# Fused attention and mixture of experts: the gates' spread earlier in GpSimd's order, two weight tiles behind the attention, four small products fewer

## The chip, the cores and the metric

One core of a Trainium2 chip runs the whole program. The metric is the device time in microseconds; a kernel is run several times and the median counts. TensorE (PE in the profile) multiplies, VectorE (DVE), ScalarE (ACT) and GpSimd (POOL) work element by element, and SyncE (SP), GpSimd and ScalarE issue DMAs, which 16 DMA engines carry out.

## The reference

Causal attention by blocks over 8 batches, 8 heads, 576 positions and a head size of 64, and then a layer of 8 experts, each of which keeps at most `capacity` = 80 of the 4608 tokens that chose it:

```python
mask = block_i >= block_j                      # blocks of 64 positions
scores = np.where(mask, q @ k.T / 8, -1e9)
x = softmax(scores) @ v                        # then reshaped to [4608, 512]
logits = x @ w_gate                            # 8 experts
expert_idx = argmax(logits); gate_w = softmax(logits)[expert_idx]
for e in range(8):
    tok_idx = the (at most 80) tokens of expert e with the largest gate_w
    h = np.maximum(x[tok_idx] @ w1[e], 0.0)
    out[tok_idx] = gate_w[tok_idx, None] * (h @ w2[e])
```

All other rows of the output are zero.

## The kernel before

**Attention.** A step of the loop in line 764 handles one pair of heads; four pairs are a batch, so 32 pairs run in software pipelining. The list `TURN` (line 35) is an order written out by hand: entry `(d, what, ...)` in step i does `what` for pair i + d, and each engine runs its own instructions in the order of the list. `scores` (L607) makes the products of q and k, `max` (L643) and `soft` (L652) the softmax on VectorE and ScalarE, `back` (L682, L690) transposes the probabilities P on TensorE, `take` (L739, L741) copies them out of PSUM, `values` (L731, L709) multiplies by v.

**Loads.** `prep 0` transposes q on VectorE (L585) and scales it on GpSimd (L588). GpSimd also issues the DMAs of `load_v` (L554 and L557, three for the pair two ahead), of `load_k` (L544, four for the pair five ahead) and of `store` and `store2` (L353, two each, x of a finished batch into the DRAM tensor `xs`). An engine runs its instructions in order, so an issue or a wait on GpSimd holds all behind it. q, zeros for the output and, later, most weights are issued by SP.

**Gates.** Once a batch is complete its gates are worked out in pieces spread over the next steps: `logits0`, `lt`, `lm`, `ga`, `gexp`, `gb`, which ends in `Gm` (L443) on VectorE. Then `gturn` (L451) on GpSimd spreads `Gm` into `sp`, one instruction of 128x320 elements, and in the following step `turn2` (L466) multiplies `sp` on TensorE, in front of `values`. In the step where `gturn` stands, its entry comes behind `load_v`, `load_k`, `store` and `store2`. The last batch does this on VectorE instead.

**Experts.** Four weight tiles of 2 MB are loaded by GpSimd during the last four steps (L304). The others are loaded by SP in four parts each (L309), in the order in which the experts need them; every part waits for the part three before it (`UNDERWAY` = 3), and `weights(n, after)` lets its n tiles wait for the DMA `after`. Line 842 loads one tile once the last store of x has landed; line 1046 loads four more once the second gather has.

**Selection.** Between attention and experts the 80 best tokens of each expert are found. Twelve "picks" (L941) multiply one-hot rows `OH`, made on VectorE and GpSimd (L936), by token numbers; behind each of the first eight picks stands a product of the identity with itself (`warm`, L751) that nothing reads. The picks' sum gives the indices `gi` (L959) and eight indirect DMAs (L952) gather the tokens' rows of `xs`; one gather of row 0, whose result is overwritten, precedes them. Then each expert runs: transposes (L1079), first product (L1066 into `ps`), second product (L1066 into `av`), transposes back (L1109), scatter (L1114).

Of the kernel before, what the change touches and what calls it, by code (L numbers as in the profile page):

```python
# [21 lines left out]
FW0, FWA, FWC, FWB = 4, 3, 1, 1  # L22
# [48 lines left out]
    (1, "soft", 4, 0),  # L71
    (0, "soft", 0, 0),
    (0, "back", "B"),
    (2, "load_v"),
    (5, "load_k"),
    (-3, "store"),
    (-4, "store2"),
    (-4, "gate", "gturn"),
    (0, "back", "A"),
    (-1, "take", "values", 0),  # L80
    (2, "prep", 1),
# [59 lines left out]
def tile_attn_moe(ctx, tc, q, k, v, w_gate, w1, w2, capacity, out, xs=None, dbg=None):  # L141
# [153 lines left out]
    def weights(n, after=None, parts=PARTS):  # L295

        nonlocal nw
        for _ in range(n):
            src, e = wlist[nw]
            w_ = wpools[nw % len(wpools)].tile([P, KP * F], F32, name="w")  # L300
            nw += 1
            wt_[src is w2, e] = w_ = w_.rearrange("p (a f) -> p a f", f=src.shape[2])
            if nw <= FW0:
                nc.gpsimd.dma_start(w_, src[e].rearrange("(a p) f -> p a f", p=P))  # L304
                continue
            view = src[e].rearrange("(a p) f -> p a f", p=P)
            na = w_.shape[1]
            for a in range(0, na, na // parts):
                load = nc.sync.dma_start(w_[:, a:a + na // parts], view[:, a:a + na // parts]).ins  # L309
                for before in ((after,) if after is not None else ()) + tuple(parts_[-UNDERWAY:][:1] if len(parts_) >= UNDERWAY else ()):  # L310
                    tc.add_manual_dep(load, before.name, mybir.DependencyInfo(
                        mybir.DependencyClass.Sync, mybir.DependencyReason.DATA))
                parts_.append(load)
# [429 lines left out]
    def warm(n, wt, after=None, w=identr, c=4):  # L743

        if not n:
            return
        with ExitStack() as order:
            if after is not None:
                order.enter_context(tc.issue_after(after.ins))
            for i in range(n):  # L750
                nc.tensor.matmul(wt[:, 0:c * P].rearrange("p (a c) -> p a c", c=P), lhsT=w,  # L751
                                 rhs=w.unsqueeze(1).broadcast_to([P, c, P]), start=(i == 0), stop=(i == n - 1))
# [7 lines left out]
    with tc.manual_schedule():  # L760
# [48 lines left out]
        bt = batches[B - 1]  # L809
# [29 lines left out]
    tw = dict(reuse_waits="tile")  # L839
    fwa = late.enter_context(tc.tile_pool(name="fwa", bufs=FWA, **right, **tw))  # L840
    wpools += [fwa] * FWA
    weights(1, bt.stored.ins)
    sel2 = late.enter_context(tc.tile_pool(name="sel2", bufs=1, **right, **tw))


# [41 lines left out]
    HOLD = 1  # L887
# [45 lines left out]
    for n_, i in enumerate((*range(NV), *range(NH, NCAND), *range(NV, NH))):  # L933
        quiet = NH <= i < NH + NQ
        with ExitStack() if quiet else tc.issue_after(counted.ins):
            made = (pool if quiet else vec).tensor_scalar(  # L936
                OH[:, i], iota_b[:, int(i >= NV)], scalar1=pen[:, i:i + 1], scalar2=cnt[:, i:i + 1],
                op0=ALU.subtract, op1=ALU.is_equal)
        if quiet:
            last_made = made  # L940
        picked = nc.tensor.matmul(pick[0:CHUNK, 0:3 * E], lhsT=OH[:, i], rhs=RI[:, i].rearrange("p k e -> p (k e)"),  # L941
                                  start=(n_ == 0), stop=(n_ == NCAND - 1))
        if n_ < 8:
            warm(1, wt[:, n_ % 2], picked, c=2)
    gi = sel2.tile([CHUNK, E], I32, name="gi")

# [4 lines left out]
    def fetch(e, index):  # L951
        return pool.indirect_dma_start(  # L952
            out=xg[e], out_offset=None, in_=xs[:, :], in_offset=bass.IndirectOffsetOnAxis(ap=index.bitcast(U32), axis=0),
            bounds_check=NTOK - 1, oob_is_err=False).ins
# [5 lines left out]
    fetches = [fetch(e, gi[:, e:e + 1]) for e in range(E)]  # L960
# [82 lines left out]
    fwc = late.enter_context(tc.tile_pool(name="fwc", bufs=FWC, **right, **tw))  # L1043
    fwb = late.enter_context(tc.tile_pool(name="fwb", bufs=FWB, **tw))
    wpools += [fwc] * FWC + [fwb] * FWB
    weights(FWA - 1 + FWC + FWB, fetches[HOLD])

    def divide(dst, src, a0=0, a1=NP):

# [309 lines left out]
```

## Time and profile before

| what | value |
|---|---|
| median of 3 runs | 431.2 us (430.88 to 433.99) |
| the profiled execution's own time | 432.01 us |
| its span, first to last instruction | 430.3 us |
| TensorE busy | 391.5 us, 91% of the span |
| ScalarE busy | 275.3 us, 64% |
| VectorE busy | 269.8 us, 63% |
| GpSimd busy | 226.1 us, 53% |
| mean granted clock of TensorE | 0.973 |

The profile is of one execution. Busy time doesn't count DMA issues, though an engine can do nothing else while it issues one. "A <- B" in a row of waits means that A stood idle until B was done; in an instruction's row the bracket gives the idle time before it. The attention takes the span up to about 309 us, the selection up to 328, the experts the rest.

### The profile page before, as it was taken

The numbers are of one execution on the slowest core, as the hardware profiler recorded it, in microseconds if no ns is written. First come the engines' busy times: TensorE is split into PE (matmuls) and PEld (weight loads), VectorE is DVE, ScalarE is ACT, GpSimd is POOL, SyncE is SP. The second block draws the span as 40 slices with busy tenths as digits, with TensorE's granted clock in tenths as the row PEclk, the third lists the DMA queues.
The fourth block names the chain that finished last, engine by engine and source line by source line (L and its number), as shares of the span: only waits on it lengthen the run. The fifth ranks groups of instructions, "written<-read, shape, count | busy, mean of one in ns | idle before, by whom it ended". The sixth has DMA issues, their size and how long they took to land.

```text
span 430.3 us, 15486 instructions
## 1 busy us (share of the span) xinstructions
PE 391.5 (91%) x6355; PEld 296.6 (69%) x6355; DVE 269.8 (63%) x583; ACT 275.3 (64%) x796; POOL 226.1 (53%) x370
## 2 busy tenths in 40 slices
PE   8999979979979996996999799999996899999892
PEld 4667747757756774774677576767663799899892
DVE  4778759958976895897789689888683122111111
ACT  2999959959995996999699799999420110111000
POOL 8787734874674588558448855653367300000001
PEclk9999989989999999999999999999999699999997
DMA  9999945995595599769769974799957999899931
GB/s 141 156 154 150 147 107 129 224 211 127 142 195 141 133 207 171 164 136 204 175 134 205 177 181 130 181 352 327 299 155 241 313 286 308 283 315 316 314 100 35
DMA packets 120060, 84.59 MB, mean 197 GB/s; under 512 B 94333, under 2 KB 96381, under 8 KB 119984
## 3 DMA queue, kind: packets, MB, share of 16 engines
q1 hardware_dynamic: 103040, 45.57, 44.9%
q0 software_dynamic: 15744, 37.68, 36.1%
q8 instruction: 52, 0.85, 0.8%
q10 hardware_dynamic: 1200, 0.30, 0.3%
q14 instruction: 24, 0.20, 0.2%
HBM read 63.38 MB, written 20.33 MB: 195 GB/s over the span
## 4 chain that ended last, share of the span: by engine, by line
PE 65%; POOL 11%; DVE 8%; DMA 6%; SPq 4%; issue 3%; ACT 1%; POOLq 0%; ACTq 0%; DVEq 0%
PE sc L731 17%; PE sc L607 14%; PE ps L1066 11%; PE av L1066 7%; PE sc L682 7%; DVE negm L643 4%; POOL ld L544 4%; SPq L544 3%; PE sc L370 2%; POOL vn L557 2%; POOL xs L353 2%; DMA vn<-in_v_dram 1%; DVE T L585 1%; PE sc L690 1%; POOL T L588 1%
## 5 line engine op out<-in xcount | busy, mean ns | idle before, releaser
L652 ACT ACTIVATE P<-sc,negm 128x320 f32<-128x320 f32 (+4 forms) x320 | 163.8, 528 | 13.0 <-DVE negm L643 7.0
L643 DVE TENSOR_REDUCE negm<-sc 128x1 f32<-128x448 f32 (+4 forms) x224 | 128.9, 624 | 22.2 <-PE sc L614 15.0
L607 PE MATMUL sc<-T,T 64*128 64x64 f32 (+4 forms) x768 | 110.6, 414 | 1.5 <-ACT T L581 0.5
L607 PEld LDWEIGHTS sc<-T,T 64*128 64x128 f32 x768 | 69.4, 187 | 33.1 <-issue 25.3
L544 POOL DMA_DIRECT2D ld<-in_k_dram x120 | 80.2, 678 | 0.0
L739 ACT COPY PT<-sc 128x1024 f32<-128x1024 f32 x63 | 60.7, 1018 | 21.9 <-PE sc L682 21.4
L588 POOL TENSOR_SCALAR T<-T 128x576 f32<-128x576 f32 x31 | 20.6, 666 | 91.8 <-DVE T L585 88.8
L652 ACT ACTIVATION_READ_ACCUMULATOR P<-sc,negm 128x1 f32 (+1 forms) x320 | 65.8, 206 | 0.0
L731 PE MATMUL sc<-PT,vn 128*64 128x128 f32 (+1 forms) x512 | 64.4, 395 | 0.6 <-issue 0.6
L682 PE MATMUL sc<-ident,P 64*128 64x64 f32 x1280 | 55.0, 227 | 0.2 <-ACT P L652 0.2
L731 PEld LDWEIGHTS sc<-PT,vn 128*64 128x64 f32 x512 | 35.5, 142 | 25.2 <-issue 25.0
L1114 POOL DMA_INDIRECT out_dram<-y,si x8 | 7.4, 930 | 79.8 <-DVE y L1110 79.8
L682 PEld LDWEIGHTS sc<-ident,P 64*128 64x128 f32 x1280 | 45.8, 138 | 4.2 <-ACT P L652 0.7
L1066 PE MATMUL ps<-xsT,w 128*64 128x80 f32 x1024 | 42.4, 242 | 6.6 <-issue 6.6
L585 DVE STREAM_TRANSPOSE T<-ld 128x576 f32<-128x576 f32 x62 | 47.4, 766 | 0.0
L1066 PEld LDWEIGHTS ps<-xsT,w 128*64 128x64 f32 x1024 | 39.6, 144 | 8.5 <-issue 7.8
L731 PE MATMUL sc<-PF,vn 64*64 64x64 f32 (+1 forms) x640 | 43.4, 254 | 0.0
L741 DVE COPY xT<-sc 128x576 f32<-128x576 f32 x32 | 23.9, 748 | 30.1 <-PE sc L709 30.1
L557 POOL DMA_DIRECT2D vn<-in_v_dram x64 | 39.9, 629 | 1.5 <-DMA vn<-in_v_dram 1.5
L1091 ACT ACTIVATE hT<-ps 128x320 f32<-128x320 f32 x16 | 7.0, 437 | 50.6 <-PE ps L1066 41.9
L731 PEld LDWEIGHTS sc<-PF,vn 64*64 64x64 f32 (+1 forms) x640 | 29.0, 137 | 10.4 <-issue 8.9
L1066 PE MATMUL av<-hT,w 128*64 128x80 f32 x896 | 32.8, 233 | 0.0
(183 smaller groups left out, 430.0 us busy)
## 6 DMA issues: line engine op xcount, KB each, us to landing
w<-in_moe_w_dram SPq DMA_DIRECT2D x48, 512.0 KB, 5.3
out_dram<-zero SPq DMA_DIRECT2D x18, 512.0 KB, 5.6
ld<-in_q_dram SPq DMA_DIRECT2D x124, 72.0 KB, 4.5
ld<-in_k_dram POOLq DMA_DIRECT2D x120, 72.0 KB, 5.1
w<-in_moe_w_dram POOLq DMA_DIRECT2D x4, 2048.0 KB, 12.8
xs<-Y POOLq DMA_DIRECT2D x28, 288.0 KB, 15.0
vn<-in_v_dram POOLq DMA_DIRECT2D x32, 128.0 KB, 4.4
vn<-in_v_dram POOLq DMA_DIRECT2D x64, 64.0 KB, 4.2
```

The costliest lines, as they stand in the source:

```text
L544: eng.dma_start(self.nat[x][r], (q, k)[x][self.b, self.h0 + h, :, 32 * i:32 * i + 32] .rearrange("(g r) d -> r g d", r=32))
L557: nc.gpsimd.dma_start(self.vn[c * BLK:(c + 1) * BLK, 1], turned[:, :, 1 - c])
L585: nc.vector.transpose(t, self.nat[x].rearrange("p g d -> p (g d)"))
L588: nc.gpsimd.tensor_scalar(t, t, scalar1=SCALE, scalar2=1.0, op0=ALU.mult, op1=ALU.mult)
L607: nc.tensor.matmul(to[h], lhsT=self.T[0][r, q:q + P], rhs=self.T[1][r, k0:k1], start=start, stop=stop)
L643: nc.vector.tensor_reduce(to, src, axis=AX.X, op=ALU.max, negate=True)
L652: nc.scalar.activation(dst, src, AF.Exp, bias=self.negm[0:n, u, h:h + 1], scale=1.0, accum_out=self.bt.sums[0:n, u, self.h0 + h:self.h0 + ...
L682: nc.tensor.transpose(pt[:, c, to(c, n_)], row[u][r, h, k(u, h, j):k(u, h, j) + P], ident[r, r])
L731: nc.tensor.matmul(to, lhsT=lhs, rhs=rhs, start=(n_ == 0), stop=(n_ == len(steps) - 1))
L739: nc.scalar.copy(*self.out.pop((what, x)))
L741: nc.vector.tensor_copy(*self.out.pop((what, x)))
L1066: yield nc.tensor.matmul(dst(b)[64 * c:64 * (c + 1)], lhsT=w_[:, a, col:col + 64], rhs=x_[:, a], start=(a == 0 and b == 0), stop=(a == n - ...
```

## The change

Three edits. In `TURN` the entry `gturn` moves from behind `store2` to the place right behind `back B`, ahead of `load_v`. Line 842 loads two tiles instead of one and no longer waits for the last store of x; line 1046 loads one tile fewer, so the order of the tiles and their buffers stay. The product behind a pick stands only behind the first four picks.

```diff
@@ TURN
     (0, "back", "B"),
+    (-4, "gate", "gturn"),
     (2, "load_v"),
     (5, "load_k"),
     (-3, "store"),
     (-4, "store2"),
-    (-4, "gate", "gturn"),
     (0, "back", "A"),
@@ line 842
-    weights(1, bt.stored.ins)
+    weights(2)
@@ line 943
-        if n_ < 8:
+        if n_ < 4:
             warm(1, wt[:, n_ % 2], picked, c=2)
@@ line 1046
-    weights(FWA - 1 + FWC + FWB, fetches[HOLD])
+    weights(FWA - 2 + FWC + FWB, fetches[HOLD])
```

On GpSimd the last instruction ahead of `load_v` in a step is the scaling of q (`prep 0`, L588).

## Rows read from the trace of the kernel before

**Rows 1.** The page, part 4: chain that ended last, shares by engine.

```profile
PE 65%; POOL 11%; DVE 8%; DMA 6%; SPq 4%; issue 3%; ACT 1%; POOLq 0%; ACTq 0%; DVEq 0%
```

**Rows 2.** Waits of TensorE, whole span: us in total, times, longest.

```profile
PE sc L466 <- POOL sp L451: 15.2, 5, 3.5
PE ps L1066 <- issue: 6.6, 8, 1.7
```

**Rows 3.** Chain in order of time, around one turn: start us, us, what.

```profile
194.83 0.07 DVE Gm L443
...
196.11 0.62 POOL T L588
...
203.56 0.81 POOL sp L451
```

**Rows 4.** Timeline of TensorE, two turns: start us, us, [idle before].

```profile
204.41 0.35 PE L466 MATMUL sc<-sp,sameR 128*32 128x40 f32 x16 [3.50 <-POOL sp L451]
...
275.71 0.35 PE L466 MATMUL sc<-sp,sameR 128*32 128x40 f32 x16
```

**Rows 5.** Windows: PE, PEld, DVE, ACT, POOL busy; PEclk; DMA share; GB/s.

```profile
204.40:241.40 37.00, 34.27 (x517) 24.74 (x517) 30.02 (x58) 31.75 (x91) 24.82 (x38) 1.00 0.81 171
241.40:275.70 34.30, 34.23 (x513) 24.69 (x513) 28.44 (x55) 29.91 (x86) 22.25 (x35) 1.00 0.69 164
89.70:93.70 4.00, 4.00 (x42) 2.65 (x38) 0.36 (x1) 0.24 (x2) 3.47 (x6) 0.57 0.89 187
```

**Rows 6.** Chain in order of time: `values` behind three other turns.

```profile
89.01 4.53 PE sc L731 x40
...
127.87 4.42 PE sc L731 x40
...
167.01 2.92 PE sc L731 x40
```

**Rows 7.** Windows of the end of the attention and behind it, columns as before.

```profile
300.00:305.00 5.00, 5.00 (x94) 3.85 (x92) 3.52 (x11) 4.47 (x14) 1.06 (x2) 1.00 1.04 391
308.50:316.50 8.00, 6.73 (x74) 4.19 (x71) 4.95 (x18) 0.94 (x3) 3.99 (x7) 1.00 0.84 159
319.50:325.50 6.00, 5.90 (x43) 3.98 (x44) 3.89 (x20) 2.94 (x15) 5.10 (x10) 1.00 0.95 351
325.50:329.00 3.50, 1.96 (x20) 0.66 (x12) 0.89 (x4) 0.23 (x1) 2.59 (x4) 1.00 0.41 127
335.20:342.20 7.00, 6.17 (x81) 5.62 (x82) 0.76 (x2) 0.86 (x2) 2.01 (x8) 0.53 1.03 296
```

**Rows 8.** Timeline of GpSimd and SP; then landing of weight parts.

```profile
294.23 1.41 POOL L353 DMA_DIRECT2D xs<-Y  x2 [0.71 <-DMA w<-in_moe_w_dram]
303.04 0.79 POOL L451 TENSOR_TENSOR sp<-Gm,sameE 128x320 f32<-128x320 f32 x1 [1.96 <-DVE Gm L443]
...
317.94 4.38 SPq L309 DMA_DIRECT2D w<-in_moe_w_dram  x4
323.09 1.11 POOL L952 DMA_INDIRECT xg<-xs,none  x1 [0.17 <-issue]
324.74 0.97 POOL L952 DMA_INDIRECT xg<-xs,gi  x1 [0.54 <-DVE gi L959]
DMA to landing us min/median/max: 4.0/5.3/7.6
```

**Rows 9.** Timeline of ScalarE around the turn at 204.41.

```profile
203.31 0.54 ACT L652 ACTIVATE P<-sc,negm 128x320 f32<-128x320 f32 x1
...
208.49 1.93 ACT L739 COPY PT<-sc 128x1024 f32<-128x1024 f32 x2 [3.58 <-PE sc L682]
```

**Rows 10.** Chain in order of time, first and last experts.

```profile
338.87 4.13 PE ps L1066 x64
...
343.42 4.58 PE ps L1066 x128
...
407.11 1.72 issue
```

## The prediction

> **What bounds the kernel now.** I read the profile's chain of work that ended last first: 65% of the span is TensorE, 11% GpSimd [rows 1]. Then the waits: TensorE's largest stands before L466, the product that turns the spread gates: 15.2 us in 5 waits, for `sp` of L451 on GpSimd [rows 2]. The reader is to see that one engine is full nearly all the time, so every gap of it that sits on the chain is time of the kernel. Third, the chain around one such wait: the gates `Gm` are done at 194.90, q is scaled from 196.11 to 196.73, but `sp` starts at 203.56, after three V issues, four K issues and two stores of x, 6.83 us behind the scaling [rows 3]; TensorE goes on at 204.41 [rows 4]. The engine was not late with work, it had work in a bad order.
>
> Fourth, the control that the trace itself holds. The last full batch has no K loads left, so its spread has four issues fewer before it, and TensorE's 275.71 shows no wait, where 204.41 shows 3.50 us [rows 4]. The stretch from turn to turn without a wait at its end lasts 34.30 us, the one before it, which ends in such a wait, 37.00; TensorE is busy 34.23 and 34.27 us in them [rows 5]. So four pairs are 34.3 us of TensorE, and a wait adds its whole length.
>
> **Part 1, the spread behind the scaling.** Nothing is added or removed; `sp` (0.81 us) passes nine DMA issues. It ends at 196.73 + 0.81 = 197.5 instead of 204.37 [rows 3], and TensorE asks for it at 204.41 − 3.50 = 200.9 [rows 4]: more than 3 us to spare. Does the spread wait in its new place, holding the DMAs behind it? Its input `Gm` is done at 194.90 [rows 3]; VectorE makes it before the transpose of the next q, and the scaling needs that transpose, so in GpSimd's order the gates are always there. Gain: the five waits, 15.2 us [rows 2].
>
> Second gain: after two of the waits the granted clock fell: 0.57 of full over 4 us behind the first [rows 5]; full speed is the 2.4 GHz level, so most of that stretch ran at 1.2 GHz. The 40 products of `values` took 4.53 and 4.42 us there (from 89.01 and 127.87), against 2.92 after the third wait [rows 6]. Without the gap there is nothing for the clock to fall for: 1.61 + 1.50 = 3.1 us.
>
> Costs: V, K and one half store are issued 0.8 us later in six batches. K is loaded five pairs ahead and V two; a pair takes 8.6 us (34.3 / 4), so this is hidden under more than a pair's work; with that cover gone it would be 6 × 0.8 = 4.8 us. Of the next scaling: GpSimd's work from one scaling to the next is at most 0.62 + 6.83 + 0.81 = 8.3 us, inside 8.6. The seventh spread has no scaling in front of it and waits for `Gm` till 303.04; the second store of that batch, now issued at 294.23, falls behind it, to 303.8 [rows 8]. Its queue still works off the POOL-issued weight tiles then (DMA share 1.04 from 300 to 305 [rows 7]), so I cost it at nothing; without that cover it adds its two issues' 1.4 us to the final stores.
>
> What is late next once TensorE no longer stops? ScalarE: TensorE would take up the turn (0.35 us) and `values` (2.92) at 200.9 and come to its transposes of P at 204.2 [rows 4, 6]. The exponentials that they need end at 203.85 [rows 9]: in time by 0.3 us, the tightest place. Now ScalarE idles 3.58 us there [rows 9]; that slack is what the change uses up. In the wait-free 34.30 us ScalarE was busy 29.91 and VectorE 28.44 [rows 5]: both fit.
>
> **Part 2, two weight tiles at once.** SP now stands at the weight loads until the last x store has landed, 317.94 [rows 8], after a stretch of the engines with x stores, share 0.84 over 8 us = 6.7 us of engine work, from 308.5 [rows 7]. One tile took 6 us at 0.95 = 5.7 us of engine work [rows 7], two take 11.4. From 308.5 stores and tiles together are 18.1 us: done at 326.6 where one tile alone was done at 325.5. If both queues share evenly, the stores end at 308.5 + 13.4 = 321.9 plus 1.5 us to be seen landed (data gone at 316.5, seen at 317.94) = 323.4; the first gather that needs them is issued at 323.09 [rows 8]: 0.3 us late, and the real gather shares its engines for at most 326.6 − 325.5 = 1.1 us more. Bounds 0 and +1.4; I take the middle, +0.7. The Trainium skill, "DMA: Bandwidth & Descriptors", section "Queues, rings and completion order", says that each engine takes turns between queues packet by packet; it speaks against this part, since wide weight packets would then hold up the stores more than evenly. By that rule the sum would lie toward the first rival below; no row here shows the two kinds side by side.
>
> What the earlier tile buys: the experts wait for no weights by name; TensorE's only unexplained gaps there are 6.6 us in 8 [rows 2], the longest 1.72 at 407.11, near the end of the loads [rows 10]. If the loads end some 6 us sooner it may go: bounds 0 and −1.7; I take −0.5, because no row shows its cause.
>
> **Part 3, four products fewer.** The first real gather is issued at 324.74, when GpSimd has stood idle 0.54 us for the index sum behind the last pick; the dummy gather in front of it ends at 324.20 whatever the picks do [rows 8]. So four products fewer gain between 0 and 0.54; part of the idle time is GpSimd's own gap between gathers, so I take 0.2. Clock: it stood at 1.00 while TensorE was busy 1.96 of the 3.50 us from 325.5 [rows 7], so a thinner half microsecond should not lower it. If it did, the next 64 products would go as they did under the slow clock of 335.2 to 342.2, 4.13 us against 2.29 at full (half of a 4.58 us group) [rows 7, 10]: +1.8. The Trainium skill, "TensorE: Matmul & The Clock Gate", "Part 1: The HAM clock gate", ties the clock to recent activity, which speaks against taking warm products away; by it alone the sum would be those 1.8 us more.
>
> **Sum.** The profiled execution took 432.0 us (430.3 span and 1.7 around it). 432.0 − 15.2 − 3.1 + 0.7 − 0.5 − 0.2 = 413.7. The median of the runs, 431.2, is 0.8 below that execution, so I give 413.0. Own range of this case: 411 to 415.5 (part 2 from −1.7 to +1.4 where the sum has +0.2, and up to a tenth of part 1 left over).
>
> **Rivals.**
> *The loads hold up the stores and the gather* (place: the 16 DMA engines between 308 and 329). If the stores are served last, they end with everything, 326.6 + 1.5 = 328.1: the gather is 5.0 us late, and after that idle stretch the first expert starts at the slow clock, +1.8. 413.0 + 6.8 − 0.7 = 419. For: equal sharing already misses by 0.3 us. Against: at most three parts of 0.5 MB are under way. Chance 0.15, spread over 416 to 420.
> *Another engine takes the wait's place*: ScalarE, with 0.3 us to spare, becomes the limit and half of part 1 goes: 413 + 9 = 422. Against: the wait-free stretch [rows 5]. Chance 0.06.
> *The experts' gap goes*: the other seven of those eight gaps, 6.6 − 1.7 = 4.9 us [rows 2], and the slow clock from 335.2 (0.53 over 7 us: 3.3 us lost [rows 7]). Another phase of loads may remove both: 413 − 8.2 = 405; the cause is unknown. Chance 0.10, spread over 404 to 410.
> *The change doesn't do what it says*: GpSimd still comes to `sp` late, since the wait is then for something else: 431, chance 0.02.
> *The other side, slower*: the weight queue starves the x stores altogether. Eight parts, three at a time, at the longest landing of 7.6 us [rows 8] are 22.8 us: 331.3; the stores then take twice their 6.7, landing at 346.2; 23.1 us late, plus 1.8: 413.0 + 24.9 − 0.7 = 437. It decides only from a landing after 341 (323.1 + the 18.2 us gained); every row so far bounds it at 328. Chance 0.02.
>
> **Numbers.** 0.65 for 413.0. Range 407 to 419: it holds the main case, three quarters of the first rival and half of the better one, 0.65 + 0.11 + 0.05 = 0.81. Faster by over 1% (about what a measurement of this kernel tells from no change) means below 426.9: 0.95; within: 0.03; slower: 0.02.
>
> **What would show it.** Right: no wait for `sp` before L466 in five batches, turns 34.3 us apart, clock 1.00 behind each; `values` at 2.92 us throughout; L309 at about 308 less 18, the gather issued some 16 us after it. Wrong: a new wait of TensorE on ScalarE's P before L682; the dummy gather waiting for stores of x; granted clock below 1 in the first expert sooner than now.

## The result and the profile after

The kernel after takes 412.6 us (median of 4 runs, 411.43 to 413.25), the kernel before beside it 432.6 (4 runs, 430.88 to 438.2): ratio 0.9547 with a 95% interval of 0.9492 to 0.9602. Ratios, here and below, leave out runs over 1.5% above the fastest of the same kernel, as the one of 438.2 is. 413.0 was forecast. The profiled execution of after took 412.99 us with a span of 411.2, against 432.01 and 430.3: 19.1 us of span went.

The page of after, the chain that ended last by engine, and two groups of part 5 (busy, mean ns of one, idle before and what ended most of it):

```profile
PE 81%; DMA 7%; SPq 3%; POOL 3%; issue 2%; DVE 1%; ACT 1%; POOLq 0%; ACTq 0%; DVEq 0%
...
L739 ACT COPY PT<-sc 128x1024 f32<-128x1024 f32 x63 | 60.7, 1018 | 3.8 <-PE sc L682 2.5
...
L682 PE MATMUL sc<-ident,P 64*128 64x64 f32 x1280 | 55.0, 227 | 0.3 <-ACT P L652 0.2
```

TensorE's share of the chain rose from 65 to 81%, GpSimd's fell from 11 to 3 [rows 1]. Waits of TensorE in after (us in total, times, longest):

```profile
PE pm L1079 <- DVE xn L1054: 5.4, 1, 5.4
PE ps L1066 <- issue: 3.8, 5, 1.3
PE sc L370 <- ACT P L652: 2.9, 1, 2.9
```

The 15.2 us for `sp` [rows 2] are gone, and a wait of 5.4 us before the first transposes of the first expert, L1079, has come. Two stretches from turn to turn in after (columns as in [rows 5]):

```profile
189.00:223.30 34.30, 34.30 (x527) 25.05 (x524) 29.84 (x59) 32.51 (x96) 24.78 (x39) 1.00 0.91 187
223.30:257.60 34.30, 34.29 (x527) 25.05 (x524) 29.83 (x59) 32.51 (x96) 24.77 (x39) 1.00 0.77 172
```

TensorE is full at full clock, and ScalarE is at 32.51 of 34.30 us: the wait-free rhythm that the control of [rows 4, 5] promised. The chain in order of time around one turn, and from the picks to the first expert (start us, us, what):

```profile
188.93 0.28 PE sc L466 x16
189.21 3.05 PE sc L731 x40
...
304.93 0.81 POOL xg L952
...
306.35 6.72 DMA xg<-xs,gi
...
313.64 0.93 PE pm L1079 x4
314.57 2.90 PE ps L1066 x39
317.47 0.32 issue
317.79 1.76 PE ps L1066 x25
319.56 0.42 PE pm L1079 x4
319.98 2.36 PE ps L1066 x64
```

The first gather, issued at 324.74 before [rows 8], is issued at 306.35, but it takes 6.72 us to land. Where the 19.1 us went, by those points:

| stretch | before, us | after, us | difference |
|---|---|---|---|
| to the sixth turn (L466) | 275.71 | 257.53 | −18.18 |
| to the issue of the first gather | 49.03 | 48.82 | −0.21 |
| to the end of the first expert's 128 products | 18.25 | 16.00 | −2.25 |
| to TensorE's last transposes | 79.89 | 81.82 | +1.93 |
| to the end of the span | 7.4 | 7.0 | −0.4 |

### The profile page after: what moved, and what is told of

Same layout as the page of the kernel before. It is cut to its first block, busy times and chain, and to the rows that moved or that the text cites. A ratio compares the mean times of both kernels' runs of the same rounds, so it can differ in the third digit from the quotient of the medians.

```text
span 411.2 us, 15473 instructions
## 1 busy us (share of the span) xinstructions
PE 387.1 (94%) x6351; PEld 296.0 (72%) x6351; DVE 268.7 (65%) x583; ACT 275.3 (67%) x796; POOL 225.9 (55%) x370
## 4 chain that ended last, share of the span: by engine, by line
PE 81%; DMA 7%; SPq 3%; POOL 3%; issue 2%; DVE 1%; ACT 1%; POOLq 0%; ACTq 0%; DVEq 0%
PE sc L731 22%; PE sc L607 21%; PE ps L1066 11%; PE sc L682 10%; PE av L1066 8%; DMA w<-in_moe_w_dram 3%; SPq L544 2%; PE sc L370 2%; PE sc L690 2%; DMA xg<-xs,gi 2%; POOL ld L544 1%; PE sc L389 1%; PE pm L1109 1%; DMA wgd<-in_moe_w_gate_dram 1%; DMA P<-in_k_dram 1%
## 5 line engine op out<-in xcount | busy, mean ns | idle before, releaser
L731 PE MATMUL sc<-PT,vn 128*64 128x128 f32 (+1 forms) x512 | 63.0, 387 | 0.6 <-issue 0.6
L588 POOL TENSOR_SCALAR T<-T 128x576 f32<-128x576 f32 x31 | 20.7, 666 | 75.5 <-DVE T L585 72.5
L731 PEld LDWEIGHTS sc<-PT,vn 128*64 128x64 f32 x512 | 37.4, 139 | 21.7 <-issue 18.9
L1066 PE MATMUL ps<-xsT,w 128*64 128x80 f32 x1024 | 41.3, 240 | 3.8 <-issue 3.8
L1066 PEld LDWEIGHTS ps<-xsT,w 128*64 128x64 f32 x1024 | 38.7, 142 | 5.6 <-issue 4.9
L1066 PE MATMUL av<-hT,w 128*64 128x80 f32 x896 | 32.7, 233 | 0.0
```

What stands on the lines that cost most here:

```text
L588: nc.gpsimd.tensor_scalar(t, t, scalar1=SCALE, scalar2=1.0, op0=ALU.mult, op1=ALU.mult)
L731: nc.tensor.matmul(to, lhsT=lhs, rhs=rhs, start=(n_ == 0), stop=(n_ == len(steps) - 1))
L1066: yield nc.tensor.matmul(dst(b)[64 * c:64 * (c + 1)], lhsT=w_[:, a, col:col + 64], rhs=x_[:, a], start=(a == 0 and b == 0), stop=(a == n - ...
```

## The experiments

Three groups of four kernels ran on three chips, on which the kernel before took 433.9 us (first four), 426.8 (next four) and 433.0 (last four; medians of 12, 7 and 5 runs, chosen as above). So only ratios, or times within a group, are compared.

**The spread alone.** The kernel before with the first edit only:

```diff
+    (-4, "gate", "gturn"),
     (2, "load_v"),
     (5, "load_k"),
     (-3, "store"),
     (-4, "store2"),
-    (-4, "gate", "gturn"),
```

> The kernel before with the first edit alone: the spread right behind the scaling of q; the weight tiles and the warm products stay as they were. Theory (the five waits and the slow clock behind two of them are the whole gain, 18.2 us): ratio to the kernel before 0.958, some 413.5 us where before is 432; the first gather lands some 3 us after its issue, as before. Rival (the early weight tile carries a good part of the gain, by the gap of the first expert that went): 417 to 420.

Measured: 413.87 us, ratio 0.9515 (0.946 to 0.9571). No wait for `sp`; the sixth turn without idle time, at 257.49, as in after. Beside this edit the other two add nothing that can be told: 0.9547 with all three, on another chip.

**Two tiles alone.**

```diff
-    weights(1, bt.stored.ins)
+    weights(2)
...
-    weights(FWA - 1 + FWC + FWB, fetches[HOLD])
+    weights(FWA - 2 + FWC + FWB, fetches[HOLD])
```

> The kernel before with the second edit alone: two weight tiles from the end of the attention, no wait for the last store of x. Theory (what it takes by the late gather, some 3.7 us, it gives back in the first expert's gap): within 1.5 us of the kernel before; the first gather lands 6 to 7 us after its issue instead of 3. Rival (it is a gain by itself): 4 us or more faster. Other rival (a loss by itself, which the spread's gain hid): 3 us or more slower.

Measured: 431.65 us, 0.9897 (0.9821 to 0.9972). The first gather was issued at 326.19 and VectorE had its data at 332.62, 6.4 us behind it, where before shows 3.1 (324.74 to 327.84): late, as in after. And yet the kernel was not slower: its interval lies just below 1, and by the medians it is 2.2 us faster, between the 1.5 that the theory allowed and the 4 of its rival. In its trace the first expert is shorter: its 128 products end 15.3 us behind the gather's issue, where before shows 18.3.

**Four products fewer alone** (`n_ < 4` for `n_ < 8`).

> The kernel before with the third edit alone: four products of the identity fewer between the picks. Theory: the first gather is issued 0.24 us earlier and nothing else moves: 0.0 to 0.5 us faster, not to be told from the kernel before. Rival (the clock falls without them): the granted clock of the first expert is below 1 from its first product, 1.8 us slower. Other rival (moving the later products by a few places changes the unexplained gap of the first expert): 2 us or more either way.

Measured: 432.9 us (8 runs), 0.9975 (0.9928 to 1.0022): nothing that can be told. In the trace the first gather waits 0.30 us instead of 0.54 [rows 8], the 0.2 that the sum had.

**The spread half-way.** The kernel after with `gturn` between `load_k` and `store`, so seven of the nine issues stand in front of it again.

```diff
-    (-4, "gate", "gturn"),
     (2, "load_v"),
     (5, "load_k"),
+    (-4, "gate", "gturn"),
     (-3, "store"),
```

> The changed kernel, but with the spread between the loads of K and the stores of x: half of the way back. Theory (every us by which the spread is late behind TensorE's arrival adds its whole length): the five waits come back shortened by the stores that no longer stand in front, 1.4, 1.4, 1.9, 1.4 and 1.4 us, 7.4 in all; 420 us where the changed kernel has 412.6, and no slow clock behind waits this short. Rival (ScalarE, which would come next, hides a short wait): below 415.

Measured: 419.37 us, 0.9641 (0.9573 to 0.9709). Its waits of TensorE:

```profile
PE sc L466 <- POOL sp L451: 7.5, 5, 1.9
PE pm L1079 <- issue: 6.2, 1, 6.2
```

Five waits again, on average 1.5 us each instead of 3.0: the two store issues, which alone changed sides, take 1.41 us [rows 8]. So a wait is as long as the issues ahead of `sp` make it, and the sixth turn comes at 265.16, 7.6 us later than in after. That settles part 1.

**What happens in the first expert.** TensorE in the timeline of before, and then GpSimd's last gather issue there:

```profile
329.14 1.58 PE L1066 MATMUL ps<-xsT,w 128*64 128x80 f32 x35
331.97 0.23 PE L1066 MATMUL ps<-xsT,w 128*64 128x80 f32 x1 [1.25 <-issue]
...
335.55 0.23 PE L1066 MATMUL ps<-xsT,w 128*64 128x80 f32 x1 [0.50 <-issue]
336.25 1.88 PE L1066 MATMUL ps<-xsT,w 128*64 128x80 f32 x24 [0.48 <-issue]
```

```profile
333.65 0.96 POOL L952 DMA_INDIRECT xg<-xs,gi  x1 [0.30 <-issue]
```

TensorE stops after some 35 of the first 64 products, does five single ones with gaps of 0.5 to 1.25 us (called the trickle below), and runs on at 336.25, 1.64 us behind the end of the last gather issue (334.61). In after, which comes there late, there is one gap of 0.32 us, and it ends at 317.79, 1.38 us behind the last gather issue (316.41). From this came theory B: TensorE can't pass that point until about 1.4 us after the last gather issue, so a late gather costs nothing. Theory A said that every late microsecond of the gather is paid.

**One tile free.** The kernel after with one tile, still without a wait for the stores.

```diff
-    weights(2)
+    weights(1)
...
-    weights(FWA - 2 + FWC + FWB, fetches[HOLD])
+    weights(FWA - 1 + FWC + FWB, fetches[HOLD])
```

> The kernel after, but with one weight tile, still without a wait for the stores, behind the attention; the other four wait for the second gather as before the change. Theory A (the second tile is what made the first gather land after 6.7 us instead of 3.0, and every late microsecond of the gather is paid): the gather lands after about 3 us, and the kernel gains the 3.7 us, about 409. Theory B (in the first expert TensorE can't pass a point at some 35 to 39 products until about 1.4 us after GpSimd's last gather issue, whenever the first gather lands): the gather lands after about 3 us, TensorE begins the expert some 3.5 us sooner, and stands there and trickles until GpSimd's last gather issue plus 1.3 to 1.6 us; the time is that of the kernel after within 1 us, 412 to 414.

Measured: 407.76 us, 0.955 (0.9511 to 0.9589). TensorE in its timeline (start us, us, [idle before]):

```profile
308.62 0.76 PE L1079 MATMUL pm<-ident,xn 80*128 80x80 f32 x4 [1.77 <-DVE xn L1054]
309.36 4.04 PE L1066 MATMUL ps<-xsT,w 128*64 128x80 f32 x64
313.33 0.50 PE L1079 MATMUL pm<-ident,xn 80*128 80x80 f32 x4
313.76 2.44 PE L1066 MATMUL ps<-xsT,w 128*64 128x80 f32 x64
```

All 64 products ran through, done at 313.40, before the last gather was even issued (313.90): on this chip theory B is wrong. The gather's data were used 3.07 us behind its issue (305.01 to 308.08).

**One tile free, gathers split.** As above, and `fetches` made in two halves, the second from a function that is called behind the first 64 products.

```diff
-    fetches = [fetch(e, gi[:, e:e + 1]) for e in range(E)]
+    fetches = [fetch(e, gi[:, e:e + 1]) for e in range(E // 2)]
...
+    def rest(mm):
+        with tc.issue_after(mm.ins):
+            fetches.extend([fetch(i, gi[:, i:i + 1]) for i in range(E // 2, E)])
+        ready(1, mm)
```

> As the run with one free tile, and GpSimd issues gathers 0 to 3 first and gathers 4 to 7 only once TensorE has done 64 products of the first expert. Theory B (the point is passed 1.3 to 1.6 us after the last gather issue that stands in front): the four issues that are left out take some 5 us, so the trickle of the first expert is about 5 us shorter: 407 to 409; a gap of the same kind may come back behind the later four gathers. Rival (the gap has nothing to do with GpSimd's gathers): it ends as long after the first products as without the split, and the time is that of the run with one free tile within 1 us.

Measured: 410.09 us, 0.9607 (0.957 to 0.9644). The edit missed its aim: GpSimd issued all eight gathers with the same 0.30 us between them, so this run says nothing about holding gathers back.

**Two tiles, gathers split** (the same edit on the kernel after).

> The kernel after, with gathers 4 to 7 issued behind the first 64 products of the first expert. Theory B: the first gather still lands after 6 us or more, since the two weight tiles are under way, TensorE comes to the point at 317 or so anyway, when the point is free, and nothing is gained: 411.5 to 413.5. If the four later gathers themselves hold up the first one's landing, it lands sooner (5 us or less) and the time falls to about 410.

Measured: 411.27 us, 0.9645 (0.9602 to 0.9689). Here, too, the gathers were issued without a break. The gather's data were used 6.24 us behind its issue (305.28 to 311.52), 3.2 us later than with one tile, and the end of the first expert's 128 products is 14.7 us behind it instead of 11.2: on this chip the late gather is paid in full at that place, as theory A says. The whole time is 3.5 us above the run with one tile, but only 1.2 above the one with one tile and the split. Those two differ by 2.3 us though their first experts are alike; of that, 1.1 us stand ahead of the first gather (305.01 against 306.11) and the rest behind the first expert, where the gaps are longer. Such differences belong to no edit that I can name, and a whole time on this chip tells the tile's price only as between 1.2 and 3.5 us.

**Twenty tiny products** ahead of the first expert, in the kernel with the spread alone.

```diff
+        warm(20, wt[:, 0], c=1)
```

> The kernel with the spread alone (the first run of this study), and 20 tiny products that nothing reads ahead of the first expert on TensorE. If the gap in the first expert belongs to a place in TensorE's own stream of instructions, it begins after about 19 of the expert's products instead of 39; if it belongs to the moment and to GpSimd, it begins at another count, at the same time. Its end, if theory B holds, stays 1.3 to 1.6 us behind the end of GpSimd's last gather issue. Time about 414 in either case, since the 20 products take under 1 us while TensorE waits for the gather.

Measured: 407.89 us in one run. The first expert has no gap here either, so its question could not be asked on this chip. What the run does show is the clock: the granted clock stays at 1.00 and the expert's first 64 products take 2.44 us, where they took 4.04 with one tile free (another kernel, without the tiny products). Of the gaps in the later experts the section on the hardware tells.

**The same chip for what is compared: the kernel after again.**

> The kernel after itself, on the same chip as the three below, as the base that they are held against. Turns 34.3 us apart, the first gather landing after 6 to 7 us.

Measured: 412.6 us (6 runs, 410.91 to 414.94), 0.9549 (0.9482 to 0.9616). Data 6.05 us behind the issue.

**The second part undone** (after with lines 842 and 1046 of before).

> The kernel after with the second part alone undone: one weight tile, which waits for the last x store. The gather lands after 3 us. Theory C (the second tile costs 3.2 to 3.7 us through the late gather, and the trickle of the first expert, 5 us, comes with the weight parts that start behind the stores, as in the kernel before and in the run with the spread alone): the trickle is back and the time is 1 to 2 us above the kernel after. Rival (the trickle hangs only on where the program's instructions lie, and four products fewer moved them): no trickle, and the time is 3 to 4 us below the kernel after.

Measured: 414.38 us (413.6 to 414.97), 0.9597 (0.9548 to 0.9647). The trickle is back and the median is 1.8 us above the kernel after, though the two spreads of runs overlap.

**One tile free and twelve tiny products** (`warm(12, wt[:, 0], c=1)` in the place of the twenty).

> One free weight tile, and 12 tiny products that nothing reads behind the last warm ones, in the 1.8 us in which TensorE waits for the first gather. In the run with one free tile the first 64 products then took 4.04 us at a clock of 0.67; with 20 tiny products in another kernel they took 2.44 at 1.00. If the clock is held, 1.6 us below the run with one free tile beside it; if 12 don't hold it, the same time.

Measured: 412.32 us (411.5 to 415.99), 0.956 (0.9491 to 0.9628): no gain. The twelve did not hold the clock: the first 33 products of the expert took 3.21 us at a granted clock of 0.50, where the run told next, without them, did 39 in 1.75 us at 1.00.

**One tile free again.**

> One free weight tile, on the same chip as the kernel after. By the gather's landing (3.0 us against 6.2 to 6.7) 3 to 4 us below the kernel after; if the gap of 407.8 to 411.3 seen against the run with split gathers belonged to that split, the same as the kernel after within 1 us.

Measured: 411.7 us (409.76 to 413.59), 0.9529 (0.9468 to 0.9591), 0.9 below the kernel after, not 3 to 4; by the number it is the other branch, but not for its reason, since the gap is in this run, too. This program ran through the first expert on the other chip; here its TensorE shows:

```profile
309.88 0.77 PE L1079 MATMUL pm<-ident,xn 80*128 80x80 f32 x4 [1.73 <-issue]
310.61 1.75 PE L1066 MATMUL ps<-xsT,w 128*64 128x80 f32 x39
313.50 0.23 PE L1066 MATMUL ps<-xsT,w 128*64 128x80 f32 x1 [1.14 <-issue]
314.21 0.23 PE L1066 MATMUL ps<-xsT,w 128*64 128x80 f32 x1 [0.48 <-issue]
...
317.10 0.29 PE L1066 MATMUL ps<-xsT,w 128*64 128x80 f32 x1 [0.34 <-issue]
317.85 1.62 PE L1066 MATMUL ps<-xsT,w 128*64 128x80 f32 x20 [0.46 <-issue]
319.40 0.80 PE L1079 MATMUL pm<-ident,xn 80*128 80x80 f32 x4
320.13 3.38 PE L1066 MATMUL ps<-xsT,w 128*64 128x80 f32 x64
```

39 products in 1.75 us, the trickle, and at 317.85 the rest, 1.70 us after GpSimd's last gather issue (ends 316.15). So theory C's condition, a weight part that starts behind the stores, is not needed for the trickle: here the tile is free. The expectations of theory A failed on this chip as those of B had on the other.

The first expert in the fourteen profiles, counted from the issue of the first gather, settles what can be settled. First, the time to the end of the expert's 128 products:

| chip | tiles that wait for no store | us from the first gather's issue |
|---|---|---|
| of the second group | one or none (three kernels) | 11.2, 11.3, 10.4 |
| of the second group | two | 14.7 |
| the others | one or none (before and five kernels) | 17.1 to 18.3 |
| the others | two (after twice, and two kernels) | 15.3 to 17.4 |

Where the trickle is absent, a gather that is 3.2 us late moves the end of the first expert by 3.5. On the other chips the late gather moves it by nothing or the other way. Second, in the nine profiles with a gap there, it ends 1.27 to 1.70 us behind the end of the last gather issue, though that issue lies anywhere between 316.0 and 336.7 us; in the half-way kernel, whose expert starts at 323.0 when GpSimd is all but through (323.9), there is no gap.

## Why the prediction was right, and where its steps were not

**Part 1 was right in mechanism and size.** Worked out: 18.3 us; measured between the same points of the two traces: 18.18, and the kernel with the spread alone shows it by itself. The control that the trace held, the sixth turn without K loads [rows 4, 5], was worth more than any reckoning of GpSimd's queue. The slow clock went with the waits: `values` takes 2.92 to 3.05 us behind each turn, with no 4.53 or 4.42 [rows 6].

**ScalarE's 0.3 us of slack was right**: transposes of P wait 0.2 us once, and the idle time of ScalarE for them, 3.58 us at one turn alone [rows 9], is down to 3.8 us before all of these copies, 2.5 of them for the transposes (the two groups of the page). With 32.51 of 34.30 us it is the next engine behind TensorE.

**The seventh spread cost nothing**, as costed. GpSimd in after:

```profile
284.90 0.79 POOL L451 TENSOR_TENSOR sp<-Gm,sameE 128x320 f32<-128x320 f32 x1 [1.95 <-DVE Gm L443]
285.64 1.38 POOL L353 DMA_DIRECT2D xs<-Y  x2
```

The store stands behind the spread's wait of 1.95 us, and the dummy gather starts at 304.93 with 0.17 us of idle time as before [rows 8], 18.16 us earlier: no store was late for it.

**Part 2's two terms were both mis-sized, and they cancel.** The gather was to share the engines for at most 1.1 us more; it landed 3.75 us later (6.72 against 2.97). The step that failed bounded its delay by the time by which all the loads together end later, 1.1 us: with stores and loads added up they were to be done at 326.6, which is 308.4 with part 1's 18.2 taken off. SP in the timeline of after up to 309, windows of after (columns as in [rows 5]), and the queues (packets, MB, share of the 16 engines) from 307 to 308 and from 311 to 312; q1 is SP's, q0 GpSimd's:

```profile
291.19 14.50 SPq L309 DMA_DIRECT2D w<-in_moe_w_dram  x8
```

```profile
291.00:299.00 8.00, 6.75 (x64) 4.25 (x61) 5.56 (x20) 0.94 (x3) 3.29 (x6) 1.00 1.00 267
...
306.00:308.00 2.00, 2.00 (x24) 0.48 (x16) 0.00 (x0) 0.00 (x0) 1.39 (x3) 1.00 0.97 322
...
313.00:317.50 4.50, 3.83 (x43) 3.26 (x43) 2.77 (x15) 0.58 (x2) 3.72 (x7) 0.50 0.79 244
317.50:319.50 2.00, 1.71 (x26) 1.62 (x26) 0.00 (x0) 0.00 (x0) 1.59 (x7) 0.58 1.01 328
319.50:325.00 5.50, 5.50 (x139) 5.23 (x140) 1.52 (x4) 1.69 (x4) 0.00 (x0) 1.00 0.98 307
```

```profile
q1 hardware_dynamic: 84, 0.29, 93.8%
...
q0 software_dynamic: 78, 0.19, 89.8%
q1 hardware_dynamic: 5, 0.01, 4.0%
```

The engines are full from the start, but the last packet of the eight parts ends at 311.6, not at 308.4: their packets, added up in the trace, took 12.9 us of engine work where the sum had 11.4 (twice the 5.7 of one tile), and from 308.2 on the gathers run among them. Of the gather's 3.75 us, 1.35 lie ahead of its queue's first packet, which comes 1.83 us behind the gather's issue instead of 0.48; this is little more than the prediction's bound. The other 2.4 come behind it, and for them the sum had no term: by 311 the loads are all but gone, and the engines are still busy, now with the gathers themselves. Until the first one lands their queue moves 0.78 MB, where before shows 0.34: the later ones, issued 1.27 us apart, have caught up with it and share the engines. That they are what holds it up fits these rows; the run that was to issue half of them later did not do so, and it stays untested.

The stores of x, which the first rival asked for, were held up, too, but nobody waited for them: their last packet ends at 301.7, 5.8 us behind the end of their last issue, where before shows 2.4, and the dummy gather is issued at 304.93. The rule of the Trainium skill, "DMA: Bandwidth & Descriptors", section "Queues, rings and completion order", that engines take turns packet by packet, which the prediction weighed, has the right direction for both: VectorE has the gather's data 3.0 to 4.0 us behind the issue with one or no free tile, 6.1 to 7.5 with two.

The other term: the experts' gaps were to shrink by 0.5 us. The first expert's did by far more: TensorE came late to the point at which the trickle of before begins, stood there 0.32 us, and had full clock from 319.50, where the trickle of before left it at 0.53 for 7 us [rows 7]. The next 64 products took 2.36 us, not 4.13 [rows 10]. From the gather's issue to the end of the 128 products the change saves 2.25 us in spite of the late gather. The later experts gave back 1.93: the gaps before L1066 there are 3.5 us against 2.2, and 0.6 I have not traced. Part 2 in all: −0.3 by these two stretches, +0.2 in the sum. That the number was right there was luck, two errors of opposite sign, and on the chip of the second group, without the trickle, the second tile moves the first expert's end by 3.5 us the wrong way.

**Part 3**: 0.2 us, as worked out; no slow clock came of it before the idle stretch. Behind that stretch, 5.4 us for the late gather, one of the prediction's own signs of being wrong did appear: the first expert starts at a granted clock of 0.50 (313.00 to 317.50), where before has 1.00 over its first 35 products (329.20 to 330.70). It cost less than the trickle had.

**The sum** has two slips that decide nothing: 0.8 below 413.7 is 412.9, and the own range's upper end comes to 416.0 by its own terms (1.2 and 1.8 above 413.0), not 415.5.

**The rivals.** The first had the right place, and the loads did hold up the stores, but by less than would have made the gather wait; the gather itself was late in landing. Its 1.8 us for a slow start did not come as a loss since the trickle of before had cost more. Of the experts' gap the prediction said that the cause was unknown and that another phase might remove it; part of it went so.

No version beats the kernel after by what can be measured: one free tile is 0.9 us below it on one chip, within the runs' spread. On the chip without the trickle it may be 1.2 to 3.5 us below; the kernel after itself was not run there.

## What to carry to other kernels

On an engine that runs in order, put the small instruction that the full engine waits for ahead of the DMA issues: each issue here held it up by some 0.7 us. Look for a step of the same loop in which the wait does not occur; it gives the gain, and shows which engine is next. When wide loads are started earlier, ask what small transfer will run beside them, and hold variants that differ by a per cent against each other on one chip, since a stall there may not exist on the next.

## What the runs showed of the hardware

**Gaps that belong to places in TensorE's own stream.** "issue" gaps in the later experts come at the same product in each kernel, moved by exactly as many products as were added in front. One such row in after, and its like in the kernels with four more (the spread alone), twelve more, and 24 more (the spread alone with twenty tiny ones); the count at xN is what is left of the group:

```profile
349.28 1.19 PE L1066 MATMUL ps<-xsT,w 128*64 128x80 f32 x27 [1.33 <-issue]
```

```profile
349.86 1.32 PE L1066 MATMUL ps<-xsT,w 128*64 128x80 f32 x31 [1.25 <-issue]
```

```profile
348.43 1.60 PE L1067 MATMUL ps<-xsT,w 128*64 128x80 f32 x39 [0.30 <-issue]
```

```profile
343.14 2.02 PE L1067 MATMUL ps<-xsT,w 128*64 128x80 f32 x51 [0.99 <-issue]
```

27 + 4 = 31, 27 + 12 = 39, 27 + 24 = 51. So the place is one in the stream of instructions, and only the length (none to 1.9 us) varies. The traces hold more on it: the page counts 52 packets of a queue named "instruction" (q8, 0.85 MB, so 16 KB each), and all 54 gaps of over 0.15 us before L1066 (L1067 where a line was added) in the later experts of the fourteen profiles end 1.2 to 1.6 us behind the end of one of them, though these packets lie some 5 us apart. The Trainium skill, "Runtime: NRT & Kernel Launch", section "Instruction fetch mechanics", says that instructions come in blocks and that crossing into the next one is mostly hidden; the places and the packets fit such borders, but the gaps are not hidden here. That ties the gaps to the fetch in time; no run changed the fetch, so that it is the cause is not shown.

**The first expert's gap is tied to GpSimd's gathers in time** (the 1.27 to 1.70 us above) in the nine profiles that have it, and absent in the four of the second group's chip, where the kernel before took some 4 to 7 us less as well (its own trace there was not taken). It is not a gap of the kind above: it does not move with the products in front. It begins behind 39 products in after and in the spread alone, which has four more in front, and behind 33, not 27, with twelve more. And the instruction queue's packet does not end it: in before the only one near ends at 331.20, and TensorE runs on at 336.25. Whether the issues cause it stays open: the edit that was to hold half of them back did not, and taking them away was not tried. Nor is it known why that chip does without it.
